# Decayed recurrence and a feed-forward layer on one core: scores and state reads as float32 products in four row groups

## The chip, the core and the metric

The kernel runs on one NeuronCore of a Trainium2 chip. The time is device microseconds of one execution. The comparison is between the median of several runs of the kernel before and of the changed one, on the same chip.

## The reference

Four batches, eight heads, 768 positions, head width D = 32 and state width N = 16. Per head a state is carried over chunks of 32 positions; the result goes through a feed-forward layer without bias.

```python
for c in range(nc):                     # chunks of 32
    cum = np.cumsum(la, axis=-1)        # la = log(clip(a))
    L = np.exp(cum[..., :, None] - cum[..., None, :]) * causal
    M = np.einsum('bhin,bhjn->bhij', Cc, Bc) * L
    y = einsum(M, xc) + einsum(Cc, state) * exp(cum)
    state = exp(sum(la)) * state + sum_j(Bc * xc * exp(cum[-1] - cum))
x = y.transpose(0, 2, 1, 3).reshape(B * S, H * D)      # 3072 x 256
h = x @ w_in                                            # 256 -> 2048
return (np.maximum(h, 0) + np.log1p(np.exp(-abs(h)))) @ w_out   # softplus, 2048 -> 256
```

All inputs of the recurrence are float32; the two weight matrices arrive as float64, read as pairs of int32.

## The kernel before

**Units.** The recurrence is cut into 24 units of 128 positions and all eight heads, i = 6 * batch + u. A unit takes these steps, each a function with a letter in the table ORDER: D `decays` (the masked decay matrix rm, on GpSimd), B `scale_b` and C `scale_c` (decayed copies bp and cc of B and C), S `score` (C times B, into PSUM tiles sp), M `weigh` (m = sp times rm, on VectorE), U `update` (four small products zp and the new state), T `spread` (tb: the state laid out against zeros, so that one product serves several heads), R `read` (tb times cc into yp), I `within` (eight products of 32 x 128, adding m times x to yp), G `grow` (y = yp times gg, and its rounded copy xh), X `rest` (xl = y - xh). gg is the growth factor; it is computed once for all positions, stored to DRAM as gd and loaded back, spread over partitions, for three units at a time.

**Scores before.** Eight heads of 16 rows share the 128 partitions. Units 0 to 3 multiply by a C that the host has laid out with zeros for the other heads (tiles head_c and head_b). Units 4 to 7 take two float32 products of 64 rows each (L334). From unit 8 on the unit's load holds B and C stacked twice, and `split_unit` makes single-pass fp32r parts of them: one ScalarE and one VectorE instruction for c_all, and again for b_rows, and two DMAs that lay c_all out into c_rows; four fp32r products of 128 x 256 follow (L339).

**Feed-forward.** Six blocks of 512 positions, each 16 steps of 128 hidden columns. A step has six fp32r products into hp (`first`: xh times w high, xl times w high, xh times w low, for two halves of the 256 inputs), softplus on ScalarE (e), its rounded copy gh, the remainder gl on VectorE, and eight steps later (LAG) six products into two accumulators (`second`). That is 96 steps of 12 products. `first_half` (H) runs the first two steps on 256 positions early, when only units 0 and 1 are done. Weights come in 16 chunks: `load_w`, then six steps each on ScalarE, VectorE and GpSimd (`split_stages`, words W) that build high and low parts wih, wil, woh, wol. Even chunks are of w_in: chunk 8 serves hidden steps 8 and 9.

**What sets the order.** The table ORDER is written by hand and fixes the front, units 0 to 3 with what is loaded around them; its instructions keep their order on every engine. What follows is planned by step: unit i starts near step 4 * (i - 4), its value part up to two steps later, and a scheduler orders the instructions of each engine. All loads run on SP's queue in program order. PSUM has eight banks: two for the accumulators, and a pool `ps` of six that hp, sp, zp, yp and a few others take in turn.

In the traces, instructions of the hand-ordered front carry line L119 (the recording helper) and loads carry L128.

Of the kernel before, what the change touches and what calls it, by code (L numbers as in the profile page):

```python
# [18 lines left out]
P = 128  # L19
# [10 lines left out]
FIRST = 8  # L30
# [3 lines left out]
U_C = U_B + NH * N  # L34
U_S = U_C + P
U_END = U_S + 2 * NQ * P
F_END = U_S + P + NQ * P

# [14 lines left out]
warm1 kc la hb lr warm7 loga logr w0 hc0 un0 un2 kb un1 W0 hc1 growth ft0 ft2 w2 B0 S0 D0 W0 hc2 fr0 fr2 B1  # L53
un3 M0 gg0 B2 W0 R0 C2 hc3 U0 W0 D1 W2 D2 gg3 U1 W0 T1 I0 C1 W2 U2 B3 w1 D3 S1 S2 un4 M1 T3 R1 T2 U3
C3 I1 G0 G1 S3 warm1 R2 gg4 M2 W2 I2 R3 warm1 W0 X1 zero M3 w6 W2 I3 W2 G3 W2 X0 w4 X3 G2 w3 un5 X2
H0 H1
# [13 lines left out]
def constants():  # L70
# [26 lines left out]
def recurrence_then_ffn(ctx: ExitStack, tc: tile.TileContext, fst, un, at, al, w_in, w_out, const, outT):  # L97
# [26 lines left out]
    nc.scalar.preload_act_table_set("natural_log_exp_and_others")  # L124

    def load(out, in_):

        tc.keep_in_program_order(nc.sync.dma_start(out, in_))  # L128

# [12 lines left out]
    def growth():  # L142
# [9 lines left out]
        load(gd.rearrange("b h (q s) -> (b h q) s", q=4), lr)  # L152


    un_s, gg_s, st = {}, {}, {}

    def load_unit(i):
        un_s[i] = p3.tile([P, U_END], F32, tag="un", name=f"un{i}")
        if i < HEAD:
            load(un_s[i][:, :U_S], fst[i, :, :U_S])  # L160
        elif i < FIRST:
            load(un_s[i][:, :F_END], fst[i])
        else:
            load(un_s[i], un[i - FIRST])

    head_b = p2.tile([P, HEAD, P], F32, tag="o1", name="head_b", bufs=1)
    head_c = {}

    def load_head_c(i):
        for g in range(2):  # L170
            rows = slice(64 * g, 64 * g + 64)
            load(head_c[i, g][rows], fst[i, rows, U_S + P : F_END])

    def load_growth(i):
        b, u = divmod(i, NU)
        if u % GU == 0:
            gg = p2.tile([P, 2, GU * P], F32, tag="gg", name=f"gg{i}")
            for g in range(2):
                src = gd[b, g * 4 : g * 4 + 4, u * P : (u + GU) * P].unsqueeze(1).broadcast_to([4, D, GU * P])
                load(gg[:, g, :], src)  # L180
            for v in range(GU):
                gg_s[i + v] = gg[:, :, v * P : v * P + P]


    c_rows = cp.tile([P, NQ, 2, P], F32R, name="c_rows")

    r_apart = [cp.tile([P, 2, NC, SUB], F32, name=f"r_apart{v}") for v in range(2)]

    def split_unit(i):
        if i < FIRST:  # L190
            return
        t = un_s[i]
        b_rows = p2.tile([P, NQ, P], F32R, tag="b_rows", name=f"b_rows{i}")

        def split(out, j):
            raw = t[:, U_S + j * NQ * P : U_S + (j + 1) * NQ * P].rearrange("p (q t) -> p q t", q=NQ)
            g, be = (kb[:, C_GB + v : C_GB + v + 1] for v in (2 * j, 2 * j + 1))
            A.activation(out, raw, AF.Copy, scale=be)  # L198
            V.scalar_tensor_tensor(out, raw, g, out.bitcast(F32), op0=ALU.mult, op1=ALU.add)  # L199

        c_all = p2.tile([P, NQ, P], F32R, tag="c_all", name=f"c_all{i}")
        split(c_all, 1)
        for e in range(2):
            rows = slice(64 * e, 64 * e + 64)
            load(c_rows[rows, :, e].bitcast(F32), c_all[rows].bitcast(F32))
        split(b_rows, 0)
        st[i] = b_rows
# [74 lines left out]
    bd = kb[:, 0 : NH // 2]  # L282
# [20 lines left out]
    def scale_b(i):  # L303
        b, u = divmod(i, NU)
        if u < NU - 1:
# [3 lines left out]
                un_s[i][:, U_B:U_C].rearrange("p (h n) -> p h n", n=N),  # L309
# [4 lines left out]
    def scale_c(i):  # L314
        b, u = divmod(i, NU)
        if u > 0:
            cc = mid[i]["cc"] = r_apart[i % 2]
            for g in range(2):
                rows = slice(64 * g, 64 * g + 64)
                (V if i in V_CC else Pl).tensor_tensor(  # L320
                    cc[rows, g],
                    un_s[i][rows, U_C:U_S].rearrange("p (c i) -> p c i", i=SUB),
                    f_row[b][rows, u, :NC].unsqueeze(2).broadcast_to([64, NC, SUB]),
                    op=ALU.mult,
                )

    def score(i, g):
        sp = mid[i]["sp", g] = ps.tile([P, 512], F32, tag="ps", name=f"sp{i}_{g}")
        if i < HEAD:
            PE.matmul(sp, head_b[:, i], head_c[i, g], start=True, stop=True)  # L330
            return
        if i < FIRST:
            rows = slice(64 * g, 64 * g + 64)
# [378 lines left out]
```

## Time and profile before

| | |
|---|---|
| runs shown | 356.24, 354.82, 356.15 us; median 356.15 |
| profiled execution | 354.56 us, of which its span 352.6 |
| mean granted TensorE clock | 0.980 |
| TensorE matmul busy | 332.8 us, 94% of the span |
| VectorE, ScalarE, GpSimd busy | 196.0, 168.4, 114.0 us |
| DMA moved | 37.23 MB, mean 106 GB/s |

A row of the timeline gives start, length, engine, source line, what is written and read, its shape and the number of records merged into it. A float32 matmul shows as two records, an fp32r matmul as one. Records of TensorE overlap: what a product takes in a stream is the distance of its start to the next one's.

### The profile page before, as it was taken

The page shows a single profiled execution, that of the slowest core. Times are in us where ns is not written, and L with a number is a line of the kernel's source. Part 1 is how long each engine was busy: PE and PEld are TensorE (multiplying, and loading weights), DVE is VectorE, ACT ScalarE, POOL GpSimd, SP SyncE. Part 2 cuts the span into 40 slices and gives each one's busy share as a digit, 9 for nine tenths or more (in the row PEclk, how much of TensorE's full clock was granted, in tenths as well). Part 3 has the DMA queues.
Part 4 walks back from the last instruction along what each step waited for, and adds up shares of the span by engine and source line. Part 5 has one row for each costly group of instructions (what it writes and reads, how often), then busy time and mean ns, then how long its engine had stood idle before and what let it go on. Part 6 is the DMA issues. An engine that isn't in the chain of part 4 may idle for free.

```text
span 352.6 us, 5070 instructions
## 1 busy us (share of the span) xinstructions
PE 332.8 (94%) x1882; PEld 252.0 (71%) x1882; DVE 196.0 (56%) x300; ACT 168.4 (48%) x297; POOL 114.0 (32%) x142
## 2 busy tenths in 40 slices
PE   6878985999999999999999999999999999999995
PEld 3533653567677877787877787787787788888884
DVE  1676999799984545553653553754363523132231
ACT  2311835584665535454644544645353534344450
POOL 6576943557631125323143322323512000000000
PEclk9689999899999999999999999999999999999999
DMA  7889745364210752141543222552303100001001
GB/s 203 222 196 335 252 136 187 120 257 144 51 70 8 214 152 91 30 135 48 162 121 109 65 82 71 140 161 93 91 30 89 31 2 0 0 23 40 0 2 59
DMA packets 22264, 37.23 MB, mean 106 GB/s; under 512 B 1632, under 2 KB 12896, under 8 KB 22240
## 3 DMA queue, kind: packets, MB, share of 16 engines
q1 hardware_dynamic: 22240, 36.91, 34.6%
q8 instruction: 15, 0.25, 0.3%
q14 instruction: 9, 0.07, 0.1%
HBM read 29.46 MB, written 3.24 MB: 93 GB/s over the span
## 4 chain that ended last, share of the span: by engine, by line
PE 76%; DMA 9%; DVE 8%; issue 2%; SPq 2%; ACT 1%; DVEq 0%; ACTq 0%
PE acc L543 33%; PE hp L503 32%; DMA wraw<-in_w_out 3%; DMA gg<-gd 3%; PE yp L407 3%; DVE w L479 2%; PE yp L393 2%; PE sp L339 2%; SPq L128 2%; DMA head_c<-in_fst 2%; DVE gl L531 1%; DMA c_rows<-c_all 1%; DVE w L477 1%; DVE w L481 1%; PE zp L364 1%
## 5 line engine op out<-in xcount | busy, mean ns | idle before, releaser
L531 DVE TENSOR_TENSOR gl<-e,gh 128x512 fp32r<-128x512 f32 x96 | 71.5, 746 | 83.0 <-ACT gh L530 82.3
L530 ACT CAST gh<-e 128x512 fp32r<-128x512 f32 x96 | 59.3, 620 | 65.2 <-PE acc L543 64.2
L503 PE MATMUL hp<-xh,wih 128*128 128x512 f32 (+1 forms) x192 | 77.2, 405 | 6.3 <-ACT wih L484 5.1
L523 ACT ACTIVATE e<-hp 128x512 f32<-128x512 f32 x96 | 56.6, 595 | 49.6 <-DVE gl L531 42.3
L543 PE MATMUL acc<-gl,woh 128*128 128x512 f32 x192 | 75.0, 390 | 0.0
L503 PE MATMUL hp<-xl,wih 128*128 128x512 f32 (+1 forms) x192 | 74.9, 391 | 0.0
L543 PE MATMUL acc<-gh,wol 128*128 128x512 f32 x192 | 74.9, 393 | 0.0
L503 PE MATMUL hp<-xh,wil 128*128 128x512 f32 (+1 forms) x192 | 74.3, 390 | 0.0
L543 PE MATMUL acc<-gh,woh 128*128 128x512 f32 x192 | 73.1, 392 | 0.2 <-DVE o L552 0.2
L503 PEld LDWEIGHTS hp<-xh,wih 128*128 128x128 f32 x192 | 36.1, 188 | 19.4 <-ACT wih L484 6.0
L292 POOL TENSOR_SCALAR_AFFINE_SELECT rm<-fc 128x1024 f32<-128x1024 f32 x20 | 32.1, 1605 | 47.8 <-DVE m L350 47.7
L543 PEld LDWEIGHTS acc<-gh,woh 128*128 128x128 f32 x192 | 36.0, 188 | 8.2 <-issue 0.8
L503 PEld LDWEIGHTS hp<-xh,wil 128*128 128x128 f32 x192 | 36.1, 188 | 8.0 <-issue 0.2
L543 PEld LDWEIGHTS acc<-gh,wol 128*128 128x128 f32 x192 | 36.0, 188 | 7.9 <-issue 0.2
L543 PEld LDWEIGHTS acc<-gl,woh 128*128 128x128 f32 x192 | 36.1, 188 | 7.5
L503 PEld LDWEIGHTS hp<-xl,wih 128*128 128x128 f32 x192 | 36.4, 189 | 6.5 <-issue 0.2
L350 DVE TENSOR_TENSOR m<-sp,rm 128x512 f32<-128x512 f32 x40 | 26.2, 684 | 14.0 <-PE sp L339 12.5
L199 DVE SCALAR_TENSOR_TENSOR c_all<-un,kb,c_all 128x512 fp32r<-128x512 f32 x16 | 17.3, 1084 | 10.4 <-ACT c_all L198 10.2
L424 POOL TENSOR_TENSOR xl<-y,xh 128x256 fp32r<-128x256 f32 x18 | 14.0, 780 | 25.8 <-ACT xh L419 25.2
L320 POOL TENSOR_TENSOR r_apart<-un,fr 64x128 f32<-64x128 f32 x32 | 17.1, 534 | 14.1 <-DMA un<-in_un 10.1
L307 POOL TENSOR_TENSOR bp<-un,ft 128x128 f32<-128x128 f32 x15 | 7.4, 491 | 42.1 <-DMA un<-in_un 23.7
L383 POOL TENSOR_TENSOR tb<-state,kb 128x128 f32<-128x128 f32 x16 | 11.9, 744 | 23.6 <-DVE state L375 23.0
(96 smaller groups left out, 306.5 us busy)
## 6 DMA issues: line engine op xcount, KB each, us to landing
un<-in_un SPq DMA_DIRECT2D x16, 768.0 KB, 4.5
wraw<-in_w_in SPq DMA_DIRECT2D x8, 512.0 KB, 7.8
wraw<-in_w_out SPq DMA_DIRECT2D x8, 512.0 KB
c_rows<-c_all SPq DMA_DIRECT2D x32, 128.0 KB, 2.4
gg<-gd SPq DMA_DIRECT2D x16, 192.0 KB
out_t<-o SPq DMA_DIRECT2D x12, 256.0 KB
un<-in_fst SPq DMA_DIRECT2D x4, 576.0 KB, 9.6
head_c<-in_fst SPq DMA_DIRECT2D x8, 128.0 KB, 6.5
```

The lines of the kernel that those rows point to most:

```text
L199: V.scalar_tensor_tensor(out, raw, g, out.bitcast(F32), op0=ALU.mult, op1=ALU.add)
L292: Pl.affine_select(out=rm.rearrange("p h c i -> p (h c) i"), in_=fc[:, u].rearrange("p h c -> p (h c)").unsqueeze(2).broadcast_to([P, NH * ...
L320: (V if i in V_CC else Pl).tensor_tensor(cc[rows, g], un_s[i][rows, U_C:U_S].rearrange("p (c i) -> p c i", i=SUB), f_row[b][rows, u, :NC]. ...
L350: V.tensor_tensor(mid[i]["m"][:, 4 * g : 4 * g + 4].rearrange("p h t -> p (h t)"), mid[i].pop(("sp", g)), mid[i]["rm"][:, 4 * g : 4 * g + ...
L383: (V if i in V_TB else Pl).tensor_tensor(tb, state[i - 1].rearrange("p (e d) -> p e d", d=D).unsqueeze(1).broadcast_to([P, 2, 2, D]), bd.r ...
L407: PE.matmul(yp[32 * hh : 32 * hh + 32, g * P : (g + 1) * P], un_s[i][:, U_X + h * D : U_X + (h + 1) * D], m[:, h, :], start=u == 0, stop=u ...
L424: (V if i in V_XL else Pl).tensor_tensor(xl[:, :, c0 : c0 + P], mid.pop(i)["y"], hi, op=ALU.subtract)
L503: PE.matmul(h[:, c0:c1], w[:, c, fs], x[:, c, c0:c1], start=i == 0, stop=i == 5)
L523: A.activation(e, h, AF.Softplus)
L530: A.copy(gh, e)
L531: V.tensor_tensor(gl, e, gh.bitcast(F32), op=ALU.subtract)
L543: PE.matmul(acc[e][:, :n], w[:, k, es], g, start=k == 0 and i == 0, stop=k == NFT - 1 and i == 2)
```

## The change

Every unit's load now holds x, B by token, B and C with (head, state) as rows, and C once more, laid out with zeros so that each group of 32 rows, two heads, gives a moving operand of 256 columns: 896 columns in place of 1536. `score` issues four float32 products of 32 rows, one for each group, into four PSUM tiles; `weigh` takes four steps of half the width. `read` issues four products of 32 rows and 64 columns into two PSUM tiles, and `grow` follows in two. `split_unit`, c_rows, head_c, r_apart and their memsets and DMAs are gone; tb is half as wide and always on VectorE. The buffers of a unit's load are four instead of three. The front's order is new; lr, gd and the first gg run on ScalarE's DMA queue; the factors of batches 2 and 3 are computed at the front's end; the load of one activation table ahead of the first ScalarE instruction is left out.

```diff
-warm1 kc la hb lr warm7 loga logr w0 hc0 un0 un2 kb un1 W0 hc1 growth ft0 ft2 w2 B0 S0 D0 W0 hc2 fr0 fr2 B1
+lr la kc un0 kb un1 w0 un2 un3 w2 w4 warm9 logr growth loga ft0 fr0 S0 D0 B0 D1 B1 M0 U0 W0 gg0 w6 S1 C1 I0 W0
...
-V_BP = (0, 2, 7)
-V_CC = (0, 1, 2, 6, 7)
-V_TB = (2, 3, 4, 6)
-V_XL = (2, 4, 7)
+V_BP = (0, 1)
+V_CC = (1, 2)
+V_XL = ()
...
-    nc.scalar.preload_act_table_set("natural_log_exp_and_others")
...
+    def load_a(out, in_):
+
+        tc.keep_in_program_order(nc.scalar.dma_start(out, in_))
...
-    def score(i, g):
-        sp = mid[i]["sp", g] = ps.tile([P, 512], F32, tag="ps", name=f"sp{i}_{g}")
-        if i < HEAD:
-            PE.matmul(sp, head_b[:, i], head_c[i, g], start=True, stop=True)
-            return
...
+    def score(i):
+
+        for q in range(NQ):
+            rows = slice(32 * q, 32 * q + 32)
+            sp = mid[i]["sp", q] = ps.tile([P, 512], F32, tag="ps", name=f"sp{i}_{q}")[:, : 2 * P]
+            PE.matmul(sp, un_s[i][rows, U_R:U_C], un_s[i][rows, U_A:U_END], start=True, stop=True)
+
+    def weigh(i):
+        m = mid[i]["m"] = p2.tile([P, NH, P], F32, tag="m", name=f"m{i}")
+        for q in range(NQ):
+            V.tensor_tensor(
+                m[:, 2 * q : 2 * q + 2].rearrange("p h t -> p (h t)"),
+                mid[i].pop(("sp", q)),
+                mid[i]["rm"][:, 2 * q : 2 * q + 2].rearrange("p h c i -> p (h c i)"),
+                op=ALU.mult,
+            )
...
     def read(i):
-        yp = mid[i]["yp"] = ps.tile([P, 512], F32, tag="ps", name=f"yp{i}")
+        yp = mid[i]["yp"] = [ps.tile([P, 512], F32, tag="ps", name=f"yp{i}_{g}")[:, :P] for g in range(2)]
         if i % NU > 0:
-            PE.matmul(
-                yp[:, : 2 * P],
-                mid[i]["tb"].rearrange("p q e d -> p (q e d)"),
-                mid[i]["cc"].rearrange("p g c i -> p (g c i)"),
-                start=True,
-                stop=False,
-            )
+            tb, cc = mid[i]["tb"], mid[i]["cc"]
+            for q in range(NQ):
+                rows, out = slice(32 * q, 32 * q + 32), slice(64 * (q % 2), 64 * (q % 2) + 64)
+                PE.matmul(
+                    yp[q // 2][out],
+                    tb[rows].rearrange("p e d -> p (e d)"),
+                    cc[rows].rearrange("p c i -> p (c i)"),
+                    start=True,
+                    stop=False,
+                )
...
-        plan(s, prepare, i)
         plan(s, attend_scores, i)
```

**TensorE, the scores of unit 8.** This is the end of the first block of positions; hp and acc are feed-forward products, sp8_g the score tiles, zp8 the state update. Before:

```order
L503 MATMUL hp0_15_882<-xl_0_304,wih_85 128x512
L503 MATMUL hp0_15_882<-xh_0_303,wil_86 128x512
L339 MATMUL sp8_0_911<-c_rows_81,b_rows8_901 128x256 x2
L339 MATMUL sp8_1_916<-c_rows_81,b_rows8_901 128x256 x2
L364 MATMUL zp8_926<-un8_735,bp8_920 32x64 x4
L543 MATMUL acc1_0_641<-gh0_8_636,wol_88 128x512
L543 MATMUL acc0_0_640<-gh0_9_666,woh_87 128x512
```

After, where sp8_0 to sp8_3 are the four row groups (rows of un8):

```order
L451 MATMUL hp0_15_927<-xh_0_215,wil_81 128x512
L283 MATMUL sp8_0_948<-un8_767 128x256
L283 MATMUL sp8_1_950<-un8_767 128x256
L491 MATMUL acc1_0_665<-gl0_8_661,woh_82 128x512
L491 MATMUL acc1_0_665<-gh0_8_660,wol_83 128x512
L491 MATMUL acc0_0_664<-gh0_9_690,woh_82 128x512
L283 MATMUL sp8_2_952<-un8_767 128x256
L283 MATMUL sp8_3_954<-un8_767 128x256
L491 MATMUL acc0_0_664<-gl0_9_691,woh_82 128x512
```

The scores stood in one piece; now three feed-forward products stand between the second and the third group. Of the 20 units from 4 on, one has its four groups in one piece, 15 have them in two (mostly three, then 1 to 14 feed-forward products, then the fourth), and four in three.

**ScalarE, the front.** lr and la are the decays by row and by token, fc, ft and fr the factors made of them, gd the growth factors in DRAM. Before:

```order
L124 ACT_TABLE_LOAD
L119 ACTIVATE la_73<-la_73 128x192
L119 ACTIVATE lr_74<-lr_74 128x192
L119 ACTIVATE w0_139<-wraw0_128 128x512
L119 ACTIVATE lr_74<-lr_74 128x192
L119 ACTIVATE fc0_153<-fp0_147 128x4x96
L119 ACTIVATE ft0_155<-fp0_147 128x96
L119 ACTIVATE fc2_163<-fp2_157 128x4x96
L119 ACTIVATE ft2_165<-fp2_157 128x96
L119 ACTIVATE fr0_186<-rp0_184 128x60
```

After:

```order
L119 DMA lr_73<-in_al 128x192
L108 ACT_TABLE_LOAD
L108 ACTIVATE lr_73<-lr_73 128x192
L108 ACT_TABLE_LOAD
L108 ACTIVATE lr_73<-lr_73 128x192
L119 DMA gd_77<-lr_73 128x192
L108 ACT_TABLE_LOAD
L108 ACTIVATE la_72<-la_72 128x192
L108 ACT_TABLE_LOAD
L108 ACTIVATE fc0_129<-fp0_123 128x4x96
L108 ACTIVATE ft0_131<-fp0_123 128x96
L108 ACTIVATE fr0_139<-rp0_137 128x60
L108 ACTIVATE w0_169<-wraw0_95 128x512
L119 DMA gg0_171<-gd_77 128x1x384 x2
```

lr now goes ahead of la, its load and the stores and loads of gd and gg stand in this queue, gg behind the rescaling of weight chunk 0, and three table loads have come between logarithms and exponentials.

**VectorE, weight chunk 8.** w8 and w5 are weight chunks on their way to wih and woh, gl0_k the remainders of the first block's hidden steps, m the weighed scores. Before:

```order
L531 TENSOR_TENSOR gl0_4_520<-e0_4_517,gh0_4_519 128x512
L417 TENSOR_TENSOR y5_568<-yp5_558,gg3_228 128x256
L486 TENSOR_TENSOR wil_86<-w10_523,wih_85 128x2x256
L531 TENSOR_TENSOR gl0_5_542<-e0_5_539,gh0_5_541 128x512
L477 TENSOR_SCALAR w8_572<-w8_572 128x512
L479 SCALAR_TENSOR_TENSOR w8_572<-wraw8_459,w8_572 128x512
L477 TENSOR_SCALAR w5_596<-w5_596 128x512
L307 TENSOR_TENSOR bp7_824<-un7_594,ft0_155 128x128
L320 TENSOR_TENSOR r_apart1_83<-un7_594,fr0_186 64x128 x2
L481 SCALAR_TENSOR_TENSOR w8_572<-wraw8_459,w8_572 128x512
```

After:

```order
L434 TENSOR_TENSOR wil_81<-w10_536,wih_80 128x2x256
L425 TENSOR_SCALAR w8_596<-w8_596 128x512
L427 SCALAR_TENSOR_TENSOR w8_596<-wraw8_499,w8_596 128x512
L425 TENSOR_SCALAR w5_620<-w5_620 128x512
L429 SCALAR_TENSOR_TENSOR w8_596<-wraw8_499,w8_596 128x512
L427 SCALAR_TENSOR_TENSOR w5_620<-wraw5_521,w5_620 128x512
L479 TENSOR_TENSOR gl0_0_392<-e0_0_389,gh0_0_391 128x512
L288 TENSOR_TENSOR m4_426<-sp4_3_424,rm4_416 128x256
L313 SCALAR_TENSOR_TENSOR state4_440<-state3_338,fr0_139,zp4_435 128x64
```

The last step of w8 stood behind the gl of hidden steps 0 to 5; it now stands ahead of the first gl.

More of the change, by code (lines that the diff above doesn't have):

```diff
@@ L33 @@
 U_B = U_X + DM
[L34 to L37, printed above, removed]
+U_R = U_B + NH * N
+U_C = U_R + P
+U_A = U_C + P
+U_END = U_A + 2 * P
 REBIAS = 2.0 ** -((1023 - 127) // 8)
@@ L151, in growth @@
         A.activation(lr, lr, AF.Exp)
-        load(gd.rearrange("b h (q s) -> (b h q) s", q=4), lr)
-    un_s, gg_s, st = {}, {}, {}
+        load_a(gd.rearrange("b h (q s) -> (b h q) s", q=4), lr)
+    un_s, gg_s = {}, {}
     def load_unit(i):
-        un_s[i] = p3.tile([P, U_END], F32, tag="un", name=f"un{i}")
-        if i < HEAD:
[L160 to L172, printed above, removed]
+        un_s[i] = p3.tile([P, U_END], F32, tag="un", name=f"un{i}", bufs=4)
+        load(un_s[i], un[i])
     def load_growth(i):
@@ L179, in load_growth @@
                 src = gd[b, g * 4 : g * 4 + 4, u * P : (u + GU) * P].unsqueeze(1).broadcast_to([4, D, GU * P])
-                load(gg[:, g, :], src)
+                (load_a if i == 0 else load)(gg[:, g, :], src)
             for v in range(GU):
                 gg_s[i + v] = gg[:, :, v * P : v * P + P]
[L185 to L190, printed above, removed]
-            return
[L192 to L207, printed above, removed]
     some = p2.tile([P, 512], F32, tag="o0", name="some", bufs=1)[:, :16].bitcast(BF16)
@@ L280, in x_parts @@
         return xparts[j], t0 - starts[j]
-    bd = kb[:, 0 : NH // 2]
+    bd = kb[:, C_BD : C_BD + 2]
     state = {}
@@ L427, in attend_scores @@
         decays(i)
-        for g in range(2):
-            score(i, g)
-            weigh(i, g)
+        score(i)
+        weigh(i)
         scale_b(i)
@@ L434, in attend_values @@
     def attend_values(i):
-        for f in (spread, update, read, within, grow, rest):
-            f(i)
+        update(i)
+        spread(i)
+        if i % NU:
+            read(i)
+        within(i)
+        grow(i)
+        rest(i)
     wih = cp.tile([P, 2, DFF], F32R, name="wih")
@@ L583, in step_w @@
         next(stages[i], None)
-    def both(f, i):
-        f(i, 0)
-        f(i, 1)
     acts = {
@@ L608, in recurrence_then_ffn @@
         "C": scale_c,
-        "S": lambda i: both(score, i),
-        "M": lambda i: both(weigh, i),
+        "S": score,
+        "M": weigh,
         "U": update,
@@ L617, in recurrence_then_ffn @@
         "X": rest,
-        "zero": lambda _: Pl.memset(c_rows.bitcast(F32), 0.0),
     }
```

112 lines of the change are left out of this document (31 added, 81 removed).

## The prediction

> **What bounds the kernel now.** I read the page's head first, then the busy time by stages, then single records of TensorE in order of time.
>
> ```profile
> span 352.6 us, 5070 instructions
> PE 332.8 (94%) x1882; PEld 252.0 (71%) x1882; DVE 196.0 (56%) x300; ACT 168.4 (48%) x297; POOL 114.0 (32%) x142
> ...
> PE   6878985999999999999999999999999999999995
> ...
> PEclk9689999899999999999999999999999999999999
> ...
> PE 76%; DMA 9%; DVE 8%; issue 2%; SPq 2%; ACT 1%; DVEq 0%; ACTq 0%
> ```
>
> ```profile
> 30.60:87.80 57.20, 49.38 (x285) 33.13 (x283) 51.79 (x75) 34.82 (x61) 33.95 (x31) 0.97 0.58 201
> 87.80:348.60 260.80, 259.76 (x1451) 206.41 (x1443) 126.81 (x191) 125.98 (x220) 60.31 (x79) 1.00 0.24 71
> ```
>
> Columns of the stages: length, then busy time of PE, PEld, DVE, ACT, POOL, then clock and DMA. From 87.8 us on TensorE is never without work (259.76 of 260.80) while VectorE and ScalarE are half idle. So in the last three quarters time is the sum of what TensorE issues, and work taken from other engines there is worth nothing. From 30.6 to 87.8 VectorE is the fullest (51.79 of 57.20) and TensorE has gaps. Ahead of that lies the head.
>
> **Prices on TensorE.** They are distances between starts, not durations, as records overlap.
>
> ```profile
> 153.20 0.39 PE L543 MATMUL acc<-gh,woh 128*128 128x512 f32 x1
> ...
> 154.56 0.64 PE L339 MATMUL sp<-c_rows,b_rows 128*128 128x256 f32 x4
> 155.03 0.40 PE L503 MATMUL hp<-xh,wih 128*128 128x512 f32 x1
> ...
> 160.27 0.39 PE L543 MATMUL acc<-gh,wol 128*128 128x512 f32 x1
> 160.59 0.32 PE L364 MATMUL zp<-un,bp 128*32 128x64 f32 x8
> 160.84 0.70 PE L393 MATMUL yp<-r_apart,tb 128*128 128x256 f32 x2
> 161.47 0.65 PE L407 MATMUL yp<-m,un 128*32 128x128 f32 x16
> 162.04 0.50 PE L503 MATMUL hp<-xh,wih 128*128 128x512 f32 x1
> 162.38 0.39 PE L503 MATMUL hp<-xl,wih 128*128 128x512 f32 x1
> ```
>
> Six FFN products fill 153.20 to 154.56: 0.227 us each. The four fp32r scores take 0.47 (154.56 to 155.03) and slip in at no further cost. The block of a unit takes zp 0.25, read 0.63, within 0.57. Ahead of it, from 160.27 to 160.59, stand 0.32 where a product needs 0.227: 0.09 to enter a tiled shape; behind it 162.04 to 162.38 is 0.34: 0.11 to leave.
>
> ```profile
> 68.61 0.39 PE L503 MATMUL hp<-xh,wil 128*128 128x512 f32 x1
> 68.93 0.43 PE L407 MATMUL yp<-m,un 128*32 128x128 f32 x8
> 69.29 0.50 PE L543 MATMUL acc<-gh,woh 128*128 128x512 f32 x1
> 69.62 0.40 PE L543 MATMUL acc<-gl,woh 128*128 128x512 f32 x1
> ...
> 75.66 0.39 PE L503 MATMUL hp<-xl,wih 128*128 128x512 f32 x1
> 75.98 1.13 PE L334 MATMUL sp<-un 64*128 64x512 f32 x4
> 77.04 0.30 PE L364 MATMUL zp<-un,bp 128*32 128x64 f32 x2
> ```
>
> A float32 product shows as two records, so x8 is four products side by side. They take 0.36 (68.93 to 69.29) and x16, eight products, 0.57: the second four cost 0.21, or 0.105 for each of their two passes over 128 columns. That is 0.21 for a pass over 256 and 0.42 over 512. The scores in two row groups (L334, 64 rows each) take 1.06; two passes of 512 alone are 0.84, both products in turn would be 1.68. So the two groups run beside each other, with 0.22 of filling and draining. **A run of float32 scores in groups of 32 rows over 256 columns** is then 2 x 0.21 + 0.22 = 0.64, however many of the four groups it holds, and with entering and leaving (0.20) 0.84 us. No row shows four groups; the ends are 0.44 (passes alone, entry free, as for the fp32r scores) and, in turn, 0.42 more for each further group. I take 0.84, since the two-group row is the nearest.
>
> The Trainium skill's TensorE: Matmul & The Clock Gate, section Measured speedup vs the span model, gives 3.07 times for four row tiles rather than 4; by that a run's passes would be 0.42 x 4/3.07 = 0.55, an estimate, and the sum 3 to 5 us more. No run here shows four row tiles.
>
> **Scores and reads, units 8 to 23.** The order says how often a run is broken. Before, the scores of these 16 units slip in whole or broken at no cost: 16 x 0.47 = 7.5. Zp 13 x 0.25 = 3.2, reads 14 x 0.63 = 8.8, within 16 x 0.57 = 9.1, and 20 tiled blocks to enter and leave, 4.0: 32.6 in all. The trace agrees: behind unit 7's block stand 1015 full products, 230.1 us, and the last record starts near 348.2.
>
> ```profile
> 83.74 0.50 PE L503 MATMUL hp<-xh,wih 128*128 128x512 f32 x1
> ...
> 348.21 0.39 PE L543 MATMUL acc<-gh,wol 128*128 128x512 f32 x1
> ```
>
> 264.7 less 230.1 is 34.6. After, the scheduler breaks nearly every unit's scores, three row groups, FFN products, then the fourth: 35 runs x 0.64 = 22.4. The read in four row groups of 128 columns costs like four within products, 15 runs x 0.36 = 5.4. Zp 3.2, within 9.6 (one unit broken), and 57 entries and exits x 0.20 = 11.4: 52.0. **Difference +19.4**; I take 18.5, since the second count may be too strict where a run follows another closely. Ends: +6 (runs at 0.44) and +23.
>
> **Units 4 to 7** are before 4 x 1.06 for scores and 12 entries, 11.9 in all; after 8 runs and 15 entries, 13.5: +1.6. Three quarters of that could hide in TensorE's gaps there; I leave it in.
>
> **The head.**
>
> ```profile
> 0.81 1.28 ACT L124 ACT_TABLE_LOAD   x1 [0.81 <-PEq L702]
> 3.95 0.26 DVE L119 TENSOR_SCALAR la<-la 128x192 f32<-128x192 f32 x1 [3.95 <-DMA la<-in_at]
> 6.56 0.26 DVE L119 TENSOR_SCALAR lr<-lr 128x192 f32<-128x192 f32 x1 [2.35 <-DMA lr<-in_al]
> ...
> 10.06 0.28 ACT L119 ACTIVATE ft<-fp 128x96 f32<-128x96 f32 x1
> ...
> 16.31 1.24 SPq L128 DMA_DIRECT2D gg<-gd  x2
> 23.76 0.76 DVE L119 TENSOR_TENSOR y<-yp,gg 128x256 f32<-128x256 f32 x2 [2.10 <-DMA gg<-gd]
> ...
> 35.89 0.50 PE L503 MATMUL hp<-xh,wih 128*128 128x256 f32 x2 [1.15 <-ACT xh L119]
> ```
>
> Before, the first y waits for gg, issued at 16.31 behind other loads on SP. After, ScalarE's own queue loads lr first (about 3.9, as la landed), stores gd and loads gg. The preload of a table with both functions is gone, so three more table loads of 1.28 stand on ScalarE: lr logarithm 4.2, scan and sum 5.3, load, exponential 6.9, gd out; load 8.3, la 8.6, load 9.9, factors done 11.0 (10.06 + 0.28 before: 0.7 later); w0's rescaling, then gg issued at 12.7 and, at the 7.4 that it took before, here in a less blocked queue 5.0 to 7.4, landed near 19.5. That is 4.2 earlier. From the first y to the last of unit 3 VectorE then issues 35 instructions: eight y at 0.28, eight m parts at 0.42, thirteen weight steps at 0.43 or 0.68, six small ones, 15.1 less some 2.4 by which neighbours overlap.
>
> ```profile
> L417 DVE TENSOR_TENSOR y<-yp,gg 128x256 f32<-128x256 f32 x20 | 8.4, 419 | 3.2 <-PE yp L407 2.2 <-POOL r_apart L320 0.9
> L119 DVE TENSOR_TENSOR bp<-un,ft 128x128 f32<-128x128 f32 x2 | 0.6, 292 | 2.2 <-ACT ft L119 2.1
> 25.63 0.68 DVE L119 SCALAR_TENSOR_TENSOR w<-wraw,w 128x512 int32<-128x512 int32 x1
> 32.89 0.43 DVE L477 TENSOR_SCALAR w<-w 128x512 int32<-128x512 int32 x1 [2.47 <-ACT w L475]
> ```
>
> The last xh follows at 19.5 + 12.7 + 0.5 = 32.7, against 35.89: **-3.2**. Ends: 0 (a weight load that blocks VectorE in order) and -8 (gg at 15).
>
> By the Trainium skill's ScalarE: Activation LUTs, section What ACT_TABLE_LOAD costs, a switch is about 2.66 us with a drain of 1.38; the head would start up to 4.1 later and the sum be about 373. The row above has 1.28, and it decides.
>
> **The gap at 61 us.** TensorE waits for chunk 8 of w_in; its last VectorE step stands behind six gl subtractions.
>
> ```profile
> 61.31 0.50 PE L503 MATMUL hp<-xh,wih 128*128 128x512 f32 x1 [3.74 <-ACT wih L484]
> ```
>
> After, those steps stand ahead of the first gl: **-3.7**. Late next would be the gl and with them the second products, which have eight steps of slack; were they late, this gain is 0.
>
> **Costed at nothing.** The split copies go:
>
> ```profile
> L199 DVE SCALAR_TENSOR_TENSOR b_rows<-un,kb,b_rows 128x512 fp32r<-128x512 f32 x16 | 18.4, 1148 | 0.0
> L199 DVE SCALAR_TENSOR_TENSOR c_all<-un,kb,c_all 128x512 fp32r<-128x512 f32 x16 | 17.3, 1084 | 10.4 <-ACT c_all L198 10.2
> L198 ACT ACTIVATE c_all<-un,kb 128x512 fp32r<-128x512 f32 x16 | 11.6, 723 | 12.7 <-DMA un<-in_un 12.5
> ```
>
> 35.7 us of VectorE and 23 of ScalarE, nearly all behind 87.8, where both have slack. The same holds for the smaller loads (DMA share 0.24), the moved tb and the halves of m and y (about +0.7 us of VectorE a unit): if VectorE were full there, they would cost 14 us.
>
> **Sum.** -3.2 - 3.7 + 1.6 + 18.5 = +13.2. The profiled execution took 354.56 us (span 352.6 and 1.96 around it), 1.6 below the runs' median of 356.15. So 367.8 for it, and 369 against the median. Ends of the likeliest case: 362 (front at its best) to 376.
>
> **Rivals.**
> - *A row group's weights load while the previous full product still streams*, so that a run costs its passes alone, 0.44. 43 runs from unit 4 on save 16, and the time is 353: faster. It decides below 0.84 - 13.2/43 = 0.53 a run. For it: the fp32r scores enter free. Against: 0.32 from 75.66 to 75.98. Chance 0.10; 0.06 that it goes halfway and ends within 0.5% (what can be told here from no change).
> - *The row groups run in turn.* 80 groups in 43 runs: 37 x 0.42 = 16 more, 385. Against: 1.06 for two groups. 0.07.
> - *PSUM.* Scores and yp take six of the six rotating banks instead of three; if the second run of a unit waits for one m part (0.42) in 23 cases, 379. Against: by the order at least seven FFN products, 1.6 us, stand between a bank's last write and its next. 0.07.
> - *The likeliest*: TensorE pays for every broken run, 369. 0.70.
>
> Faster 0.10, within 0.5% 0.06, slower 0.84. From 355 to 380 all but 0.10 at the faster end, 0.07 at the slower and a little of the likeliest's tail are held.
>
> **What would show it.** Right: TensorE without gaps from about 83 us on; starts of a score run and of the product behind it 0.64 apart, whether three groups or one; reads at 0.36; gg landed before 20; first full product near 33; no wait for wih above 1 us. Wrong: score runs at 0.45, or growing with their groups; waits on m or e ahead of scores; a first full product before 28 or after 36.

## The result and the profile after

The changed kernel takes 395.04 us (median of four runs, 394.16 to 397.22) against 356.19 before: 1.110 times the time, 95% interval 1.103 to 1.117. The forecast was 369, between 355 and 380: the sign was right, the size was not.

The head of the page after, with the rows of TensorE and its clock:

```profile
span 393.8 us, 5304 instructions
...
PE 369.7 (94%) x2097; PEld 262.5 (67%) x2097; DVE 179.7 (46%) x349; ACT 154.3 (39%) x268; POOL 86.0 (22%) x102
...
PE   5967698998999999999999999999999999999995
...
PEclk9555569698999999999999999999999999999999
```

TensorE is again busy for 94%, which by itself says nothing. The change shows in the clock's row: 0.5 in the second to fifth slice, 10 to 49 us, and 0.6 in the sixth and the eighth, where before one slice was at 0.6 and the others at 0.8 or more. Here are three stages (length; busy PE, PEld, DVE, ACT, POOL; clock; DMA share; GB/s), cut at the first full product and behind unit 7's block. As in the prediction, the first full product is the first feed-forward product that needs the last xh of the head:

```profile
0.00:47.40 47.40, 32.18 (x199) 19.21 (x199) 27.49 (x57) 14.92 (x25) 19.07 (x27) 0.59 0.67 214
47.40:105.10 57.70, 53.27 (x283) 35.18 (x283) 47.52 (x77) 30.67 (x55) 24.15 (x21) 0.83 0.30 98
105.10:390.00 284.90, 284.23 (x1620) 208.09 (x1616) 104.67 (x216) 108.73 (x189) 42.82 (x56) 1.00 0.12 37
```

Before, the same cuts lie at 35.89 and 83.74; its middle stage, for units 4 to 7:

```profile
35.80:83.80 48.00, 42.78 (x244) 28.46 (x244) 44.88 (x65) 31.54 (x56) 28.69 (x26) 0.96 0.54 181
```

The span grew by 41.2 us, 393.8 less 352.6: 11.6 in the head (47.4 for 35.9), 9.8 in units 4 to 7 (57.6 for 47.8), 19.4 behind them (19.1 when both are counted with the same number of feed-forward products), and the rest behind the last product. The forecast had -3.2, -2.1 and +18.5. So the part that it worked out most closely came out within a microsecond, and nearly all the error is in the first 105 us.

**The steady part.** TensorE's rows of a unit, in order of time; what a run takes is the distance to the next start:

```profile
135.40 0.71 PE L283 MATMUL sp<-un 32*128 32x256 f32 x8
136.04 0.50 PE L491 MATMUL acc<-gh,woh 128*128 128x512 f32 x1
...
204.33 0.45 PE L334 MATMUL yp<-cc,tb 32*64 32x128 f32 x8
204.71 0.64 PE L350 MATMUL yp<-m,un 128*32 128x128 f32 x16
...
210.04 0.71 PE L283 MATMUL sp<-un 32*128 32x256 f32 x6
210.68 0.50 PE L491 MATMUL acc<-gh,woh 128*128 128x512 f32 x1
...
213.40 0.69 PE L283 MATMUL sp<-un 32*128 32x256 f32 x2
214.02 0.50 PE L491 MATMUL acc<-gh,wol 128*128 128x512 f32 x1
```

Four row groups take 0.64 us (135.40 to 136.04), three 0.64, one 0.62: the groups do run side by side, and a unit whose scores are issued as three and one pays twice. The read takes 0.38. In the last stage TensorE's 0.67 us without work, of 284.90, all lie behind its last product: until then it doesn't stand still.

**The head.** TensorE's rows where it stood still:

```profile
8.90 2.45 PE L108 MATMUL fp<-la,kc 128*128 128x96 f32 x10 [3.90 <-ACT la L108]
...
21.08 2.58 PE L108 MATMUL sp<-un 32*128 32x256 f32 x6
27.04 1.22 PE L108 MATMUL sp<-un 32*128 32x256 f32 x2 [3.38 <-DVE y L108]
...
47.44 0.79 PE L451 MATMUL hp<-xh,wih 128*128 128x256 f32 x2 [1.64 <-ACT xh L108]
```

Unit 2's last score waits for a PSUM bank that yp of unit 1 holds until y is formed, and y waits for gg. From the chain of waits of the first 60 us (start, length, what):

```profile
6.77 5.87 DMA gd<-lr
...
13.98 12.69 DMA gg<-gd
...
29.68 0.67 ACT w L423
...
35.09 1.41 POOL wol L434
36.52 0.67 ACT w L423
...
43.32 1.52 DVE w L425
```

Two things fill it. gd takes 5.87 us to land, and the second half of gg another 12.69, to 26.67. From there to the last xh at 46.99 the chain goes back and forth over weight steps on ScalarE, VectorE and GpSimd. Lines L423 to L434 are steps that the scheduler set there; the table's own carry L108. One kind of step on VectorE takes 0.43 us when GpSimd stands still and about 1.5 beside a GpSimd instruction, and two of these three wait for ScalarE:

```profile
30.38 1.48 DVE L425 TENSOR_SCALAR w<-w 128x512 int32<-128x512 int32 x1 [1.20 <-ACT w L423]
...
37.22 0.43 DVE L425 TENSOR_SCALAR w<-w 128x512 int32<-128x512 int32 x1 [1.85 <-ACT w L423]
...
43.32 1.51 DVE L425 TENSOR_SCALAR w<-w 128x512 int32<-128x512 int32 x1
```

GpSimd is at rm from 30.30 to 31.57 and from 43.27 to 44.55, and at nothing from 36.85 to 39.16.

**Units 4 to 7.** TensorE's waits from 47.4 to 105.1 (total, times, longest), and two neighbouring products in that stage:

```profile
PE yp L350 <- DVE m L288: 1.8, 2, 1.1
PE hp L451 <- ACT xh L108: 1.6, 1, 1.6
PE sp L283 <- ACT e L471: 1.1, 1, 1.1
...
90.75 0.63 PE L451 MATMUL hp<-xl,wih 128*128 128x512 f32 x1
91.18 0.63 PE L451 MATMUL hp<-xh,wil 128*128 128x512 f32 x1
```

The products stand 0.43 us apart, where 0.227 is the pace at full clock. Of the 124 products over 512 columns in this stage 23 last about 0.6 us or more; before it was 2 of 125. Added up by the distance to the next start, waits apart, the stage's products over 512 columns take 36.1 us for 32.0 before, those over 256 columns 3.2 for 1.6, the scores 6.0 for 4.1, the reads and within products 6.5 for 4.0, and the waits 4.4 for 5.1. With 0.5 from two smaller groups (rp, zp), that is the whole 9.8.

### The profile page after: what moved, and what is told of

The parts are those of the page before. It is cut to its first block, busy times and chain, and to the rows that moved or that the text cites. A ratio compares the mean times of both kernels' runs of the same rounds, so it can differ in the third digit from the quotient of the medians.

```text
span 393.8 us, 5304 instructions
## 1 busy us (share of the span) xinstructions
PE 369.7 (94%) x2097; PEld 262.5 (67%) x2097; DVE 179.7 (46%) x349; ACT 154.3 (39%) x268; POOL 86.0 (22%) x102
## 4 chain that ended last, share of the span: by engine, by line
PE 76%; DVE 11%; DMA 5%; ACT 3%; issue 2%; POOL 2%; ACTq 0%; DVEq 0%
PE acc L491 34%; PE hp L451 31%; PE sp L283 6%; DMA gg<-gd 3%; PE yp L350 3%; DVE w L427 2%; DVE w L429 2%; PE yp L334 2%; DMA gd<-lr 1%; DVE w L425 1%; ACT w L423 1%; DVE gl L479 1%; PE zp L302 1%; DVE m L288 1%; DMA lr<-in_al 1%
## 5 line engine op out<-in xcount | busy, mean ns | idle before, releaser
L451 PE MATMUL hp<-xl,wih 128*128 128x512 f32 (+1 forms) x192 | 77.2, 402 | 0.0
L491 PE MATMUL acc<-gl,woh 128*128 128x512 f32 x192 | 76.8, 400 | 0.0
L451 PE MATMUL hp<-xh,wil 128*128 128x512 f32 (+1 forms) x192 | 76.4, 398 | 0.0
L491 PE MATMUL acc<-gh,woh 128*128 128x512 f32 x192 | 76.3, 405 | 0.0
L245 POOL TENSOR_SCALAR_AFFINE_SELECT rm<-fc 128x1024 f32<-128x1024 f32 x20 | 28.6, 1432 | 113.4 <-DVE m L288 113.2
L288 DVE TENSOR_TENSOR m<-sp,rm 128x256 f32<-128x256 f32 x80 | 31.4, 419 | 42.1 <-PE sp L283 42.1
L491 PEld LDWEIGHTS acc<-gh,woh 128*128 128x128 f32 x192 | 36.1, 188 | 13.1 <-issue 6.3
L451 PEld LDWEIGHTS hp<-xl,wih 128*128 128x128 f32 x192 | 37.5, 195 | 8.5 <-issue 1.5
L491 PEld LDWEIGHTS acc<-gh,wol 128*128 128x128 f32 x192 | 36.1, 188 | 10.5 <-issue 3.6
L283 PE MATMUL sp<-un 32*128 32x256 f32 x160 | 31.0, 437 | 1.1 <-ACT e L471 1.1
L283 PEld LDWEIGHTS sp<-un 32*128 32x128 f32 x160 | 13.3, 187 | 15.9 <-issue 9.6
L363 ACT CAST xh<-y 128x256 fp32r<-128x256 f32 x20 | 8.1, 407 | 39.6 <-DVE y L361 39.3
L350 PE MATMUL yp<-m,un 128*32 128x128 f32 x320 | 15.6, 286 | 1.8 <-DVE m L288 1.8
```

The source lines that it names most:

```text
L245: Pl.affine_select(out=rm.rearrange("p h c i -> p (h c) i"), in_=fc[:, u].rearrange("p h c -> p (h c)").unsqueeze(2).broadcast_to([P, NH * ...
L283: PE.matmul(sp, un_s[i][rows, U_R:U_C], un_s[i][rows, U_A:U_END], start=True, stop=True)
L288: V.tensor_tensor(m[:, 2 * q : 2 * q + 2].rearrange("p h t -> p (h t)"), mid[i].pop(("sp", q)), mid[i]["rm"][:, 2 * q : 2 * q + 2].rearran ...
L350: PE.matmul(yp[g][32 * hh : 32 * hh + 32], un_s[i][:, U_X + h * D : U_X + (h + 1) * D], m[:, h, :], start=u == 0, stop=True,)
L363: A.copy(xh[:, :, c0 : c0 + P], y)
L451: PE.matmul(h[:, c0:c1], w[:, c, fs], x[:, c, c0:c1], start=i == 0, stop=i == 5)
```

## Experiments on the steady part

The theory: TensorE pays 0.84 us for each broken run of scores. The kernel after breaks them because the pool `ps` has six banks and a unit's scores want four. The Trainium skill (TensorEngine Tiling (Array Packing), section Restrictions and Gotchas) says that different row tiles can't write the same bank at once, hence the four; no run here tried it otherwise.

**whole.** TensorE in the order of the code from unit 8 on:

```diff
...
+        pe_in_order[0] = s >= (8 - HEAD) * NFT // 4
```

> After, with TensorE's instructions behind unit 7 in the order of the code: the four score products of each unit 8 to 23 stand in one piece (16 runs instead of 35, and 32 tiled blocks instead of 57). Theory (a run costs 0.64 us whatever its number of row groups, and 0.20 to enter and leave): 19 runs x 0.64 + 25 x 0.20 = 17.2 us less behind unit 7, about 378 us. Rival (row groups cost by the group): about 5 us less, for the entries alone, 390. Second rival (six PSUM banks: in this order TensorE waits for m parts or for e): waits of 0.5 us or more a unit show ahead of the scores or products, and the time is 385 or more. The front to unit 7 stays as in after: first full product near 47.

388.25 us. The other work behind unit 7 (the time from there to the end of the last product, less 0.2267 for each FFN product) fell from 53.9 to 47.7 us, 6 of the 17 expected. A row of the waits view and two of the timeline show where 10 went:

```profile
PE hp L110 <- DVE m L290: 7.4, 13, 0.6
...
208.24 0.71 PE L110 MATMUL sp<-un 32*128 32x256 f32 x8
...
209.52 0.50 PE L110 MATMUL hp<-xh,wih 128*128 128x512 f32 x1 [0.57 <-DVE m L290]
```

The next hp wants a bank while all four still wait for m: the second rival holds beside the theory, and the time is in its range.

**whole_early.** Scores between the first and the second products of a step:

```diff
...
+        early = [x for x in fills[s] if x[0] is attend_scores and s >= (8 - HEAD) * NFT // 4]
+        for f, args in early:
+            f(*args)
         values(s)
...
```

> As the run with whole scores, but each unit's four scores are issued between the six first products of a step and its six second products, which need no rotating bank. In the run before, the first product behind the scores waited 0.57 us a unit for a part of m (7.4 us in 13 waits, 10.1 with those of yp and zp). Theory (the broken runs cost 17 us, and the wait for a bank took 10 of the gain): the waits on m go, as 1.4 us of second products lie between the scores and the next bank that is wanted; 378 to 381 us. Rival (VectorE frees the banks later than that in any case): waits on m of 0.3 us or more stay ahead of hp, yp or zp in most units, 384 to 388.

390.11 us, and 48.0 of other work: no better, and in neither range. The waits on m are gone, but the fourth score's weights now wait for a bank that softplus is reading:

```profile
PEld sp L110 <- ACT e L473: 7.1, 15, 0.5
```

**scores_mid.** Scores between the two halves of the second products, 0.68 us behind the last hp and 0.68 ahead of the next:

```diff
...
         for e in range(2):
+            if e == 1:
+                for f, args in between:
+                    f(*args)
...
```

> As the two runs with whole scores, but the four scores stand in the middle of a step's six second products: three of them (0.68 us) ahead, three behind. With none behind, the next first product waited 0.57 us for m; with none ahead, the fourth score waited 0.5 us for the bank that the softplus was still reading. Theory (a broken run costs 0.84, and it was the six PSUM banks that made the scheduler break them): both waits go, the time behind unit 7 that is not FFN products falls from 53.9 to 37 to 40 us, and the time is 379 to 382. Rival (with four banks for scores one of the waits stays in any order): 45 or more, and 386 to 390.

377.78 us. The first product behind unit 7, one unit's scores, and the last product:

```profile
103.93 0.50 PE L453 MATMUL hp<-xh,wih 128*128 128x512 f32 x1
...
200.66 0.80 PE L110 MATMUL sp<-un 32*128 32x256 f32 x8
201.38 0.50 PE L110 MATMUL acc<-gh,woh 128*128 128x512 f32 x1
...
371.33 0.39 PE L110 MATMUL acc<-gh,wol 128*128 128x512 f32 x1
```

267.4 us, less 1014 products of 0.2267, leaves 37.5 (37.9 counted to the end of the last). Both waits are gone, and 16 us with them; the time is 1.2 us below the range. Scores that stood in 35 runs now stand in 16, and 57 tiled blocks have become 31: 17.4 us at the prediction's prices. A whole run takes 0.72 us here (200.66 to 201.38) instead of 0.64, which is most of the difference. So it is shown that the breaks cost about what the prediction said. That it was the four banks of six that made the scheduler break the scores fits the waits of the two runs before, but no run gave it more banks.

These three runs have after's head. Their first full product came at 48.5, 48.3 and 45.1 us, so a difference of one or two microseconds in it says nothing.

## Experiments on the head

**oldorder.** After's bodies, before's order and queues and its preloaded table, S2 and S3 moved behind the y that frees their banks:

```diff
...
+warm1 kc la lr warm7 loga logr w0 un0 un2 kb un1 W0 growth ft0 ft2 w2 B0 S0 D0 W0 fr0 fr2 B1
+un3 M0 gg0 B2 W0 C2 U0 W0 D1 W2 D2 gg3 U1 W0 T1 I0 C1 W2 U2 B3 w1 D3 S1 un4 M1 T3 R1 T2 U3
+C3 I1 G0 G1 S2 warm1 R2 M2 W2 I2 S3 warm1 W0 X1 M3 w6 R3 W2 I3 W2 G3 W2 X0 w4 X3 G2 w3 un5 X2
+H0 H1
...
```

> After's bodies (row-group scores and reads, no split copies, loads of 448 KB) with a head in before's order and on before's queues: all loads on SP, the table preloaded, ft2 and fr2 early, warm products in two pieces; S2 and S3 moved behind the y that frees their banks. Theory (the 26 us that the prediction missed come from the order of the head and what it does to gg and to the clock): first full product at 34 to 38, unit 7's block ends near 85 to 88, time 373 to 379. Rival (they come from the bodies: four banks for scores, two for yp, eight m and y parts): first full product after 44 and 388 us or more.

386.69 us, first full product at 42.6, no y waiting for gg: 8 us back, between the two. This head is still 6.7 us longer than before's. VectorE stands still in it for 3.9 us ahead of a weight step that the scheduler set before unit 2's m, on a chunk that had not landed:

```profile
27.13 0.66 ACT L426 ACTIVATE w<-wraw 128x512 f32<-128x512 f32 x1 [3.17 <-DMA wraw<-in_w_out]
27.82 0.43 DVE L428 TENSOR_SCALAR w<-w 128x512 int32<-128x512 int32 x1 [3.88 <-ACT w L426]
```

**gg_first**, w2, w4 and w6 behind gg3:

```diff
-lr la kc un0 kb un1 w0 un2 un3 w2 w4 warm9 ... W0 gg0 w6 S1
+lr la kc un0 kb un1 w0 un2 un3 warm9 ... W0 gg0 gg3 w2 w4 w6 S1
...
```

> After, with the head's loads of w2, w4 and w6 put behind gg3 on SP's queue, so that they start only when gd is stored. Theory A (gg's late landing, 22.1 and 26.7, holds TensorE in unit 2's scores and moves the whole head): gd is stored before 11, gg0, still issued near 12.7 behind w0's rescaling on ScalarE, lands by 18; unit 2's scores take 1.3 us in place of 7.1, the first full product starts at 39 to 42, and the time is 387 to 391. Rival B (the weight steps on VectorE and ScalarE between the y set the first full product): gg lands early, but the first full product stays at 45 to 48 and the time at 393 to 396. Rival C (w2 and w4, now late, hold VectorE in order): first full product after 48.

396.67 us, a miss: gg0's second half was used at 27.4 (26.7 in after). gg3 was issued at 12.5, just ahead of gg0 at 12.7, and the three chunks from 13.7 on; that these took gg0's share of the DMA engines is likely, but nothing in this run sets it apart.

**gg3_late**, gg3 behind H1 in the table:

> After, with the load of gg3 (needed for unit 3's y, near 45 us) moved on SP's queue from behind w6 to behind the half products of the head. Theory (gg3's 384 KB, let go at the same moment as gg0 and first in its queue, hold up gg0, whose packets start only at 16 and end at 26.7): gg0's packets start by 14 and its second half lands by 20; unit 2's scores take 3 us or less; the first full product comes at 40 to 44, and the time is 388 to 392. Rival (gg0 is slow by itself, or through the weights' loads): it lands after 24, and the time is 393 to 397.

389.29 us, but gg's second half was only used at 26.1. The edit had not done what it was meant to: SP's queue keeps its own order alone, w1 went out at 8.7 instead of 13.9, and gg3 was issued at 12.9 all the same. The first full product came at 46.6; most of the gain lies in units 4 to 7 (52.1 us for 57.6), and what caused it there was not tested. So it was done again.

**gg3_behind**, gg3 behind un5:

```diff
-... R1 gg3 w1 D2 ... X2 W2 un5 R3 I3
+... R1 w1 D2 ... X2 W2 un5 gg3 R3 I3
```

> After, with gg3's load behind un5 on SP's queue (un5 waits for unit 1's buffer), so that it is issued after 20 us; the run before had put it behind w1 alone and it was still issued at 12.9. w1 and w6 are as early as there. Theory (the reads of gd, each row 32 times, move some 95 KB a us in all, and gg3 takes half of that from gg0): gg0's second half lands by 20 instead of 26.2, unit 2's scores take 3 us or less, the first full product comes at 40 to 44, and the time is 383 to 388. Rival (ScalarE's queue moves some 45 KB a us whatever else is there): it lands at 23 to 27, first full product at 45 to 48, 388 to 391.

390.63 us: gg landed at 21.5 instead of 26.7, first full product at 42.3; the time missed its range by 2.6 and lies in the rival's, though the landing came ahead of the rival's. The DMA view from 16 to 20 us (queue: packets, MB, share), first of after, then of this run; q10 is ScalarE's, q1 SP's:

```profile
q1 hardware_dynamic: 292, 0.52, 45.6%
q10 hardware_dynamic: 110, 0.17, 12.4%
```

```profile
q10 hardware_dynamic: 242, 0.36, 25.1%
q1 hardware_dynamic: 85, 0.18, 17.5%
```

With SP's queue full, gg came at 0.17 MB in 4 us; with it nearly empty, at 0.36. The Trainium skill (DMA: Bandwidth & Descriptors, section Queues, rings and completion order) has each DMA engine take turns between queues packet by packet; by that a queue of its own gives the urgent load a share, not precedence, and these rows agree in that, though the share was not an equal one (110 packets to 292).

**weights_behind.** The weight steps that the table doesn't name are pinned behind the head:

```diff
 def split_w(step):
+    in_order[0] = True
     for _ in split_stages(step):
         pass
+    in_order[0] = False
```

> After, with the weight steps that the table doesn't name put behind the head's instructions on VectorE, ScalarE and GpSimd, where the scheduler had set nine of their VectorE steps (5.4 us) among the head's. Theory (the chain from gg's landing at 26.7 to the last xh at 47 runs through these steps): the first full product starts at 40 to 42, and the time is 387 to 391. Rival (they are wanted as soon as the products run): the first full product comes at 40 to 42, but TensorE waits for wih and woh for several us between 45 and 90, and the time is 393 to 398.

388.43 us. The first full product starts 8.6 us earlier, at 38.9, and before the range expected. The time is in the theory's range, but the rival's waits came too: TensorE waits 7.5 us for parts of w_in before 96 us:

```profile
PE hp L453 <- POOL wil L108: 4.0, 1, 4.0
PE hp L453 <- ACT wih L108: 3.5, 3, 1.8
```

**warm33.** More warm products at the start and ahead of S2:

> After, with 33 warm products in place of 9 at the start and 10 more ahead of unit 2's scores; they compute nothing that is used. Theory (half clock is a cause of its own: 0.50 from 12 to 57 us): TensorE is at full clock from about 5 us on, fp takes 1.2 us in place of 2.45, the first products of H0 and H1 start 0.12 apart in place of 0.21, the first full product comes at 43 to 45, and the time is 388 to 392. Rival (the half clock follows from the waits for gg and for VectorE): the clock is back at 0.5 by 30 us, first full product at 46 to 48, time 393 to 397.

390.60 us. fp took 1.35 us, but H0 and H1 still ran at half pace and the first full product stayed at 47.3: in the head the rival is right. The gain came later; only 9 of the 124 products of units 4 to 7 were slow, instead of 23.

**table_only**, the preload restored:

```diff
+    nc.scalar.preload_act_table_set("natural_log_exp_and_others")
...
```

> After with the table of logarithm and exponential preloaded, and nothing else: three table loads of 1.28 us go, two of them ahead of the factors. Theory (the head is set by gg's landing and the weight steps behind it): gd is issued 1.3 us earlier, gg lands at 25 to 27 as before, and the time is 393 to 396. Rival (the table loads set the head's start): la's logarithm and all behind it 2.6 us earlier, 391 to 392.5.

**ft_only**, ft2 and fr2 behind fr0:

> After with ft2 and fr2 (the ten fp products, sums and rp of batches 2 and 3) behind ft0 and fr0 as before, and nothing else; in after they stand on TensorE from 43.2 to 49.5, right around the first full product. Theory (the first full product waited for xh at 47.4, not for them; only rp's 0.7 us wait and 2 us of half-clock work behind it go): 393 to 396. Rival (they are on the path with all of 4.9 us): 390 to 392.

392.34 and 390.69 us, both at the rivals' numbers but not by the rivals' way: the first full product stayed at 47.2 and 48.2. In both, fewer products of units 4 to 7 were slow, 7 and 0 of 124. At 0.20 us each, 23 fewer are 4.6 us, about ft_only's gain. That is as far as it goes: no run set the clock alone.

**head_all**, the edits of gg3_behind, weights_behind, table_only and ft_only together, and 33 warm products at the start:

> After, with all the suspects of the head changed together: weight steps that the table does not name behind the head's, gg3 behind un5, the table with both functions preloaded, ft2 and fr2 behind ft0 and fr0, 33 warm products. Theory (gg's late landing and the weight steps in the chain are the 15 us by which the first full product came late): first full product at 32 to 36, unit 7's block at 86 to 90, 379 to 383. Rival (what is left is the VectorE work of the bodies): first full product after 38, 386 or more.

380.47 us, as expected, with the first full product at 34.2, near where the prediction had put it. Units 4 to 7 still take 54.0 us, 6 more than before the change.

## Both together, and before with a part of the change

**combined** (head_all and scores_mid) and **combined_two** (of the head only gg3 and the weight steps):

> After with the scores in the middle of a step's second products and all the head's edits (weight steps behind the head, gg3 behind un5, table preloaded, ft2 and fr2 early, 33 warm products). Theory (the two causes lie in different stretches and add): 395.5 less 17.7 less 15.0 is 363, between 361 and 365; first full product near 34, unit 7's block near 88, 37 to 39 us behind it that are not FFN products. Rival (they overlap, or the order of the code brings new waits in units 4 to 7): 367 or more.

> As the run with both, without the preloaded table, the early ft2 and fr2 and the 24 further warm products: of the head's edits only gg3 behind un5 and the weight steps behind the head are left. Theory (these two carry the head): at most 4 us more than the run with all, 363 to 367. Rival (table, clock and fp2 are each worth 2 us or more): 369 or more.

366.97 and 370.77 us, ratios 1.034 (1.026 to 1.041) and 1.043 (1.037 to 1.048). The first is outside the theory's range and at the rival's. The causes don't add in full: 4 us are missing, of which 2 are other work behind unit 7 (39.7 against 37.9 in scores_mid). TensorE's waits in combined, 34 to 105 us:

```profile
PE hp L457 <- ACT wih L110: 7.7, 4, 4.7
PE hp L457 <- POOL wil L110: 2.4, 3, 1.8
```

The products come sooner than their weights: there are gaps for w_in again, 10.1 us here and 7.5 in head_all. Two things do this, and no run tells them apart: the head is shorter, and the weight steps pinned behind it come later (the third part of wih is ready at 48.7 us here and at 43.7 in after). oldorder, with a first full product at 42.6 and nothing pinned, has no such gap. And combined_two falls to its rival: the table, ft2 and the warm products are worth 3.8 us together.

**before_rowread.** Before, with row-group reads from unit 8 on and all else as it was:

```diff
...
+        if i >= FIRST:
+            read_rows(i)
+            return
...
```

> Before, with one part of the change alone: from unit 8 on the reads are four products in four row groups of 128 columns (two banks, y in two halves), scores as before. Theory (a read costs 0.36 in place of 0.63): 14 reads save 3.8 us less some 0.4 where two are broken: 352.5 to 353.5 against 356.4. Rival (the read in the full array entered free between the two tiled pieces, or the second yp bank brings a wait): 355.5 to 358.

354.19 against 355.84 us, ratio 0.9962 (0.9937 to 0.9987): the only version faster than both kernels, by 0.4% and between theory and rival. Before's own median lay between 355.15 and 356.48 from one comparison to the next, so it is a small gain. Behind unit 7 the profiled execution has 34.4 us of other work for 34.8. Fourteen reads fell from 7.6 to 6.1 us on TensorE, not by 3.8: before, a read had cost 0.54 on average, not the 0.63 of the one row that I took, and TensorE's other work is cut into 40 pieces for 36.

**before_mid.** The same with TensorE in the order of the code, scores in the middle, split copies three steps earlier:

> Before with row-group reads from unit 8 on, and TensorE behind unit 7 in the order of the code, with the scores of a unit in the middle of a step's second products and the split copies three steps earlier. Theory (broken blocks cost TensorE 0.20 and a run each, in this kernel too: 40 pieces where some 30 would do): the time behind unit 7 that is not FFN products falls from 34.4 to 29 to 31, and the time from 354.2 to 349 to 351.5. Rival (the scheduler's order covered waits for the copies' DMA or for m): waits of 0.3 us or more a unit on c_rows or m, 354 to 358.

365.85 us, ratio 1.028 (1.025 to 1.032), a miss: other work rose from 34.4 to 45.5, of which 10.6 are waits. The longest, and what held ScalarE ahead of it:

```profile
PE yp L123 <- ACT e L565: 2.9, 1, 2.9
...
134.64 0.72 ACT L202 ACTIVATE c_all<-un,kb 128x512 fp32r<-128x512 f32 x1 [4.20 <-DMA un<-in_un]
```

The copy, now three steps earlier, stands ahead of e on ScalarE and waits 4.20 us for its unit's load. So this wait comes from the earlier copies as much as from TensorE's order, and the run doesn't tell the two edits apart. Even without its waits the other work would be 34.9 us, where before_rowread has 33.3 without its own: joining 40 tiled pieces to 32 saved nothing here.

Start of the first full product, start of unit 7's last products, and other work behind that, all in us:

| run | us | first full product | unit 7's last products | other work behind |
|---|---|---|---|---|
| before | 356.2 | 35.9 | 83.5 | 34.8 |
| after | 395.0 | 47.4 | 104.9 | 53.9 |
| scores_mid | 377.8 | 45.1 | 103.7 | 37.9 |
| weights_behind | 388.4 | 38.9 | 95.5 | 54.2 |
| gg3_behind | 390.6 | 42.3 | 99.4 | 53.9 |
| ft_only | 390.7 | 48.2 | 99.1 | 53.9 |
| head_all | 380.5 | 34.2 | 88.0 | 54.3 |
| combined | 367.0 | 34.4 | 88.4 | 39.7 |

## Why the prediction was right and wrong

- **Units 8 to 23, +18.5: right, +19.1.** A run of 0.64 whatever its groups, 35 runs and 57 tiled blocks as counted, reads at 0.38 for 0.36, entries and exits: all seen in rows, and scores_mid took 16 us of it back by joining the runs. Both counts were too low by 1.5 to 2 us, 52.0 for 53.5 after and 32.6 for 34.4 before, and that cancels in the difference.
- **Rivals.** Row groups in turn: wrong, four take as long as one. Weights loaded under the previous product: wrong, no run below 0.62. PSUM: no waits in after, as the prediction argued, but by whole and whole_early it and the likeliest case are one cause: scores left in one piece wait for banks. The argument looked for waits and not for what the scheduler had done to avoid them.
- **The head, -3.2: wrong, +11.6.** Two terms failed. The first is "landed near 19.5". gg was issued at 12.7 as forecast, though by another way: gd, which took 5.87 us, landed only at 12.64, and gg3 on SP, which has no rescaling ahead of it, was let go at the same moment. The second half of gg was issued at 13.98 and took 12.7 us instead of 5.0 to 7.4; the queue that was called less blocked shared the DMA engines with everything that SP had waiting, and gg3_behind brought the landing from 26.7 to 21.5. The second is the 12.7 us for "35 instructions". The count was right, 35 with thirteen weight steps, nine of them the scheduler's. Their price was not: they were added up back to back at the lengths that they have undisturbed. From 26.7 to the end of the last y, 46.5, VectorE waited 3.05 us for the weights' ScalarE steps, and the rest took 16.8 us; the steps that took longer than undisturbed all overlap an instruction of GpSimd. To the last xh it was 20.3 instead of 12.7. That is 7.2 and 7.6 of the 27.8 us by which the profiled execution missed its forecast of 367.8. With the scheduler's steps moved away, weights_behind has its first full product 8.6 us earlier. The ends of this term, 0 and -8, were argued from VectorE and from a faster landing; none let gg land later than before.
- **Units 4 to 7, +1.6, and the gap at 61 us, -3.7: wrong by 11.9.** No wait for wih was left in after, but the reason given carries little of that: chunk 8 of w_in was ready at 59.2 us, only 2.0 earlier than before, while TensorE came to hidden step 8 at 79.0 instead of 61.3. That the gap went is mostly the lateness of the products, and so luck for this term. Waits for m, xh and e took its place (4.4 us of idle TensorE against 5.1 before), and products and tiled work at half pace cost more: of the 9.8 us, 5.7 are feed-forward products. The sum had no term for the clock.
- **Costed at nothing: right for the steady part**, where VectorE is busy 104.67 of 284.90 us. In units 4 to 7 it is busy 47.52 of 57.70, and the halves of m and y stand in that queue; what they cost there was not measured apart.
- **ft2 and fr2 behind the head** were left out of the count. They did not delay the first full product, but the stage behind it: with them early, ft_only takes 4.4 us less, and none of that stage's products is slow.

## What to carry to other kernels

Price a small tiled product by the run, and ask how many runs the scheduler will make of it: here the waits point to the number of free PSUM banks, and an issue point with unrelated work on both sides took these waits away. When a stretch is priced by counting one engine's instructions, follow the chain through the other engines too: the count of 35 was right, and waits for ScalarE and steps beside GpSimd still made it more than half as long again. Price a load by all that is let go with it. Put a term for the clock wherever an engine order opens waits on TensorE.

## What was not expected of the hardware

TensorE's pace fell to half after short waits. At the start the nine warm products stand 0.427 us apart, which is already half pace: in warm33 they are 0.216 apart from the eleventh on. The granted clock of after reads 1.00 from 5.3 to 8.7 us, while TensorE stood still from 5.0 to 8.9, and 0.50 from 8.7 to 12.0, and fp ran at 421 ns a record against 275 before. The Trainium skill (TensorE: Matmul & The Clock Gate, section What's actually happening) gives one idle window of about 3.4 us for such a fall, and this agrees. But near 88 us it fell again with no wait longer than 1.12. There two waits together took 1.8 of 3.4 us (window, length, busy TensorE, clock, DMA share, GB/s):

```profile
87.20:90.60 3.40, 1.59 (x26) 1.00 0.00 0
90.62:94.03 3.41, 3.41 (x9) 0.50 0.45 135
```

From 53.1 to 56.5 TensorE is busy for 2.60 of 3.41 us, and the clock is 0.50 in the next 3.4 us; from 66.7 to 70.1 for 2.39 of 3.44, with the same result. So waits seem to count by their sum within such a stretch. It isn't a full rule: from 70.1 to 73.5 TensorE is busy throughout, and the clock stays at 0.50 until 76.9.

The granted clock on the page isn't always to be trusted: in ft_only it reads full speed where fp takes the same slow 2.45 us as in after.

```profile
PEclk9999999999999999999999999999999999999999
...
9.06 2.45 PE L108 MATMUL fp<-la,kc 128*128 128x96 f32 x10 [4.06 <-ACT la L108]
```

The distance between the starts of equal products is the better measure.
